# An attention step in another order, with its loads further ahead

## The chip, the cores and the metric

The kernel runs on one core of a Trainium2 chip. The metric is the device time of one execution in microseconds (us).

## The reference

An mLSTM cell and an expert layer follow each other. For 4 batches, 8 heads, 768 positions and head width 40, the cell carries a 40 x 40 matrix C, a vector n and a running maximum m:

```python
for t in range(S):
    m_new = np.maximum(f_gate[:, :, t] + m, i_gate[:, :, t])
    f_stab = np.exp(f_gate[:, :, t] + m - m_new)
    i_stab = np.exp(i_gate[:, :, t] - m_new)
    C = f_stab * C + i_stab * einsum('bhd,bhe->bhde', vt, kt)
    n = f_stab * n + i_stab * kt
    y[:, :, t] = sigmoid(o_gate[:, :, t]) * (C @ qt) / max(abs(n . qt), 1)
```

The cell's output, as 3072 rows of 320 values, goes through one of 8 experts per row, chosen by a hash of the row's token id:

```python
for e in range(8):
    mask = (token_ids * 2654435761) % 8 == e
    out[mask] = np.maximum(x[mask] @ w1[e], 0) @ w2[e]      # 320 -> 1024 -> 320
```

## The kernel before, in words

Attention works on tiles of 128 positions of one batch with all 8 heads: 6 chunks by 4 batches, 24 steps; step s has batch s % 4 and chunk s // 4. Inside a tile the recurrence is written as a masked product of scores and decays; between chunks C (with n as its 41st column) is carried, two buffers per batch. Each engine takes its instructions in the order in which the program issues them, and that order is written out by hand. Of a step there are these parts:

- `turn` (L300): four PE transposes of k, four of q, each into a PSUM tile of tag `tr`; ScalarE copies them to kT and qT, or VectorE in the step after a sigmoid.
- `decays` (L308): four matmuls of L with R (gate rows, loaded from DRAM) give the exponents `ab`, ScalarE takes their exponential into w; two more matmuls give `xb`, the decay of the row against the chunk's start, also in a `tr` tile; VectorE makes qs = qT * xb (L328), ScalarE copies the last column into `dec`.
- `decayed` (L358): GpSimd multiplies the old C by `dec` into the other buffer of C.
- `state` (L366): the update. PE makes k^T v into the last 164 columns of a PSUM tile `xh`, VectorE adds it to C (L381; in the first chunk a copy, L379).
- `k_weights` (L332): GpSimd makes kw, the weighted k of the update.
- `scores` (L346): 16 matmuls of kT and qT into two PSUM tiles; VectorE multiplies them into w (L354).
- `attend` (L383): the output. PE adds qs times the old C and w times v into the first 328 columns of the same `xh`; VectorE makes the denominators `den` from it (L402 to L404).
- `divided` (L406): VectorE divides into x. `gated` (L411): GpSimd multiplies x by the output gate, after a sigmoid over 8 steps at once (steps 5, 12 and 19). `store` (L415): to rows in DRAM.

In step s the order before is: decayed(s), divided(s-1), turn(s+2), decays(s+1), state(s), k_weights(s+1), scores(s+1), gated, attend(s). The gate preparation of chunks 1 to 4 (`g1`) hangs on steps 0 to 2, that of chunk 5 (`g2`) on steps 13 and 14. Routing hangs on the steps too, in `pieces`: iotas in 2 and 3, counts, totals, extra tiles, ranks and slots in 4 to 9, `route_hot` (one-hot tables on VectorE and GpSimd) in 10 to 17, `route_table` (six matmuls into `tk`, also a `tr` tile, and their sum into tv) in 12, 14, 16 and 18, and the index in 20. The first expert's weights are loaded on the way in seven slices, in the odd steps from 9 to 21.

PSUM has two buffers of tag `tr` in rotation, shared by the k and q turns, xb, tk and the small transposes; a new tile waits until the one before last has been read. SP issues nearly all loads, in order, and waits where a buffer isn't free: k and q are loaded 4 steps ahead into 4 buffers, v 3 ahead, and the gate rows R 2 ahead into 3.

Experts then follow on PE: gathers of rows on GpSimd, transposes, layer 1 (L760, L767), layer 2 (L796), a scatter. Each expert's weights are three tiles, with three buffers in `wpool` and in `w2pools[0]`; a second pool for w2 of three more is opened after attention, on the memory that attention gives back. Weights of expert 0 are loaded during attention, those of 1 and 2 on ScalarE's queue in the first expert.

Of the kernel before, what the change touches and what calls it, by code (L numbers as in the profile page):

```python
# [14 lines left out]
ALU = mybir.AluOpType  # L15
# [7 lines left out]
def kernel(  # L23
# [52 lines left out]
    consts = ctx.enter_context(tc.tile_pool(name="consts", bufs=1))  # L76
    wpool = ctx.enter_context(tc.tile_pool(name="wpool", bufs=3))
    w2pools = [ctx.enter_context(tc.tile_pool(name="w2pool", bufs=3))]

# [6 lines left out]

    def weights(src1, src2, w2pool, eng=None):
# [14 lines left out]
    def load_weights(e, eng=None):  # L102

        W[e] = weights(moe_w1[e], moe_w2[e], w2pools[e // 3 % 2], eng)

    def slices_of(e):

        w1t = wpool.tile([P, 2, F], F32, name="w1t")
        w1c = wpool.tile([P, FB // 2, P], F32, name="w1c")
# [21 lines left out]
    with tc.tile_pool(name="gates", bufs=1) as gp, \  # L131
# [5 lines left out]
        assert NB == 6 and BH == 32 and 3 * H <= 32 and DP == HB  # L137
        NG = 8
        ks = [gp.tile([P, H, DP], F32, name=f"k{i}") for i in range(4)]
        qs = [gp.tile([P, H, DP], F32, name=f"q{i}") for i in range(4)]  # L140
        vs = [gp.tile([P, H, D1], F32, name=f"v{i}") for i in range(4)]
        kws = [gp.tile([P, H, DP], F32, name=f"kw{i}") for i in range(2)]
        Cs = [[gp.tile([P, PR, 2, D1], F32, name=f"C{b}{i}") for i in range(2)] for b in range(B)]
        Ls = [gp.tile([P, B, P], BF16, name=f"L{i}") for i in range(2)]
        Lx = gp.tile([P, HB], BF16, name="Lx")
        Rs = [gp.tile([P, 2, H, P], BF16, name=f"R{i}") for i in range(3)]
        f_sb = gp.tile([BH, S], F32, name="f_sb")
# [21 lines left out]
        def load(s, what, eng=None):  # L169
            d = st.setdefault(s, {})  # L170
            eng = eng or nc.sync
            if what == "o":
                if s % NG == 0:
                    og[s // NG] = ld.tile([P, NG, H, D], F32, name="og", bufs=2)
                eng.dma_start(og[s // NG][:, s % NG], rows_of(o_gate, s))
            else:
                bufs, src = {"k": (ks, k), "q": (qs, q), "v": (vs, v)}[what]
                d[what] = bufs[s % 4]
                eng.dma_start(d[what][:, :, :D], rows_of(src, s))
# [6 lines left out]
        def load_a(s):  # L186
            n = 3 if s < B else 6
            src = pieces_of(s)[:, :n].rearrange("h i t -> i h t")
            for i in range(2):
                nc.sync.dma_start(Rs[s % 3][32 : 32 + n, i], src)  # L190

# [108 lines left out]
        def turn(s, what, on_act=True):  # L300
            d = st[s]
            d[what + "T"] = wk.tile([P, PR, P], F32, name=what + "T", bufs=3)
            tp = ps.tile([P, PR, P], F32, name="tr", tag="tr", bufs=2)
# [4 lines left out]
        def decays(s):  # L308
            b, c = place(s)
            d = st[s]  # L310
            R, L = Rs[s % 3], Ls[c % 2]
            w = d["w"] = wk.tile([P, 2, PR, P], F32, name="w")
# [70 lines left out]
        def attend(s):  # L383
# [4 lines left out]
            for j in range(PR):  # L388
# [6 lines left out]
                for hf in range(2):  # L395
                    for t in halves:
                        nc.tensor.matmul(  # L397
                            hs[t, 2 * j + hf, :], lhsT=d["w"][:, hf, j, t], rhs=d["v"][:, 2 * j + hf, :],
                            start=(c == 0), stop=True, skip_group_check=True,
                        )  # L400
            den = d["den"] = wk.tile([P, H, 1], F32, name="den")
            nc.vector.tensor_scalar(den[:], hs[:, :, D:], scalar1=-1.0, scalar2=1.0, op0=ALU.mult, op1=ALU.max)  # L402
            nc.vector.tensor_tensor(den[:], den[:], hs[:, :, D:], op=ALU.max)
            nc.vector.reciprocal(den[:], den[:])  # L404

        def divided(s):  # L406
            d = st[s]
            d["x"] = wk.tile([P, H, D], F32, name="x", bufs=8)
            nc.vector.tensor_tensor(d["x"][:], d["hs"][:, :, :D], d["den"][:].to_broadcast([P, H, D]), op=ALU.mult)

# [161 lines left out]
        def route_index():  # L572
# [11 lines left out]
            8: [lambda: route_beyond(CAP, b2), route_chosen], 9: [route_slots], 20: [route_index],  # L584
        }
        for i in range(NT // TH):
            pieces.setdefault(12 + 2 * i, []).append(lambda i=i: route_table(i))
        for i in range(2 * NT // TH):
# [29 lines left out]
        load_a(1)  # L618
        nc.vector.tensor_tensor_scan(m_sb[:, 1:], f_sb[:], i_sb[:], NEG, op0=ALU.add, op1=ALU.max)
        load(1, "v")  # L620
        load_a(2)
        for c in range(1, NB - 1):
            nc.sync.dma_start(m1[(c - 1) * BH : c * BH, :], m_sb[:, c * P : (c + 1) * P + 1])
        turn(1, "k")
        turn(1, "q")
        g0.weights(kwT0)
# [6 lines left out]
        nc.gpsimd.tensor_copy(Lx[:], one[:, 1].to_broadcast([P, HB]))  # L633
        load(3, "k")
        load(3, "q")
        load(2, "v")
        decays(0)
        scores(0)
        nsig, ndone, waiting = -1, 0, []
        for s in range(NT):  # L640
            b, c = place(s)
            if s + 2 < NT and s > 0:
                load_a(s + 2)
            if b == 2 and c < NB - 1:
                load_e(c + 1)
            if s + 4 < NT:
                load(s + 4, "k")
            if s + 3 < NT:
                load(s + 3, "v")
            for i in o_at.get(s, ()):  # L650
# [5 lines left out]
            waiting = []  # L656
            decayed(s)
            if s > 0:
                divided(s - 1)
            if s + 2 < NT:  # L660
                turn(s + 2, "k", s - 1 not in sig_at)
                turn(s + 2, "q", s - 1 not in sig_at)
            if s + 4 < NT:
                load(s + 4, "q")
            if s + 1 < NT:
                decays(s + 1)
            state(s)
            if s + 1 < NT:
                k_weights(s + 1)
                scores(s + 1)  # L670
            for i in range(2):
                if ndone < s and ndone // NG <= nsig:
                    gated(ndone)
                    waiting.append(ndone)
                    ndone += 1
            attend(s)
            if s in sig_at:
                nsig = sig_at[s]
                sigmoid(nsig)
            if s == 0:  # L680
                g1.sums(False)
                g1.split("A")
                g1.rows("A", nc.scalar.copy)
                nc.scalar.dma_start(z1[:, :3], g1.zt[:, :3])
            if s == 1:
                nc.scalar.activation(g1.t["X"][:, 0], g1.t["A"][:, 0], AF.Exp)
# [4 lines left out]
                g1.split("X")  # L691
                g1.rows("X", nc.scalar.copy)
                nc.scalar.dma_start(z1[:, 3:6], g1.zt[:, 3:6])
            if s == 2:
                g1.weights(kwT1)
            if s == 13:
                g2.sums(False)
                g2.split("A")
                g2.rows("A", nc.scalar.copy)
                g2.ends()  # L700
                g2.split("e")
                g2.rows("e", nc.scalar.copy)
            if s == 14:
                nc.scalar.activation(g2.t["X"][:, 0], g2.t["A"][:, 0], AF.Exp)
                g2.split("X")
                g2.rows("X", nc.scalar.copy)
                nc.scalar.dma_start(z2[:], g2.zt[:])
            for piece in pieces.get(s, []):
                piece()
        divided(NT - 1)  # L710
        while ndone < NT:
# [162 lines left out]
    with tc.If(nx > 0):  # L874
        with tc.For_i(0, nx, 1) as k:
# [5 lines left out]
                moe_w1[bass.ds(ex, 1)].rearrange("e d f -> (e d) f"),  # L881
                moe_w2[bass.ds(ex, 1)].rearrange("e f d -> (e f) d"), w2pools[0],
            )
# [37 lines left out]
```

## Time and profile before

| | |
|---|---|
| Time of three runs | 416.63, 416.9, 417.96 us (median 416.9) |
| The profiled execution's own time | 416.36 us |
| Its span in the trace | 414.6 us |
| PE busy | 371.1 us, 90% of the span |
| VectorE, ScalarE, GpSimd busy | 144.5, 104.6, 122.8 us |
| First output matmul of step 4 | 45.60 us from the span's start |
| First output matmul of step 23 | 149.77 us |
| First matmul of the experts | 165.79 us |

PE stands for the matmul engine, DVE for VectorE, ACT for ScalarE, POOL for GpSimd, SP for the engine that issues most DMAs. In the page's slices a digit is the busy share of a fortieth of the span in tenths. A row of the timeline has start, duration, engine, line, operation, output and inputs, the number of instructions merged, and in brackets how long the engine stood idle before it and who ended that. The chain of waits has start, duration and what ran. A row of stretches has its limits, its length, the busy time of PE, weight loads, DVE, ACT and POOL with the number of instructions, the clock granted to PE, the DMA engines' busy share and GB/s.

### The profile page before, as it was taken

Reading aid. Unit: us, or ns where it says so; the run is one execution under the profiler, and the core shown is the slowest. Engines: PE = TensorE matmul, PEld = TensorE weight load, DVE = VectorE, ACT = ScalarE, POOL = GpSimd, SP = SyncE. Lnnn points to the kernel's source line nnn. Section 1 sums busy time; section 2 is a strip of 40 time slices with the busy share of each in tenths; the row PEclk is TensorE's granted clock in tenths of the full one; section 3 lists DMA queues with packets and bytes.
Section 4 is the critical chain, followed back from the end, with each engine's and each line's share of the span. In section 5 each row is a group of like instructions: output and inputs, shape, how many; then the busy total and the mean of one; then the engine's idle time right before and its main releaser. Section 6 shows DMA issues by size and latency. Waiting matters only on the chain.

```text
span 414.6 us, 7819 instructions
## 1 busy us (share of the span) xinstructions
PE 371.1 (90%) x3124; PEld 251.8 (61%) x3124; DVE 144.5 (35%) x392; ACT 104.6 (25%) x203; POOL 122.8 (30%) x202
## 2 busy tenths in 40 slices
PE   4677998896899963999999999999999999999992
PEld 2565887785777751557566566556566565575561
DVE  8283888888777752110110200200200201101100
ACT  6334472464444810010110111110111110101100
POOL 5614255144762426301402313012313112010020
PEclk9996998999999995799999999999999999999997
DMA  7496987998399813998235254144254100000000
GB/s 148 79 171 129 178 149 152 206 200 158 79 213 191 212 68 96 300 288 268 63 112 174 79 171 146 32 144 148 61 171 146 33 17 30 0 32 17 0 18 32
DMA packets 125206, 50.91 MB, mean 123 GB/s; under 512 B 105164, under 2 KB 121424, under 8 KB 125168
## 3 DMA queue, kind: packets, MB, share of 16 engines
q1 hardware_dynamic: 117296, 36.36, 37.9%
q0 software_dynamic: 2496, 8.20, 6.4%
q10 hardware_dynamic: 5376, 5.84, 4.7%
q8 instruction: 25, 0.41, 0.4%
q14 instruction: 13, 0.11, 0.1%
HBM read 42.03 MB, written 8.61 MB: 122 GB/s over the span
## 4 chain that ended last, share of the span: by engine, by line
PE 71%; issue 8%; DVE 7%; POOL 5%; DMA 4%; ACT 2%; SPq 1%; POOLq 0%; ACTq 0%; DVEq 0%
PE mh L767 23%; PE zp L796 22%; PE mh L760 6%; PE xh L397 4%; PE tr L305 3%; PE sp L352 3%; PE xh L391 3%; PE ab L316 2%; POOL x L413 1%; PE tp L743 1%; PE xh L375 1%; PE zp L837 1%; DMA L<-gate_pieces 1%; POOL oh_c L554 1%; DMA R<-gate_pieces 1%
## 5 line engine op out<-in xcount | busy, mean ns | idle before, releaser
L796 PE MATMUL zp<-w2t,h 128*128 128x320 f32 x384 | 105.2, 433 | 0.0
L767 PE MATMUL mh<-xT,w1t 128*128 128x416 f32 x256 | 98.8, 530 | 0.9 <-POOL xT L829 0.9
L796 PEld LDWEIGHTS zp<-w2t,h 128*128 128x128 f32 x384 | 72.7, 190 | 32.1 <-issue 3.3
L767 PEld LDWEIGHTS mh<-xT,w1t 128*128 128x128 f32 x256 | 47.8, 194 | 44.0 <-issue 41.6
L749 DVE COPY xT<-tp 128x384 f32<-128x384 f32 x16 | 8.9, 558 | 142.3 <-PE tp L745 142.3
L730 POOL DMA_INDIRECT out_dram<-zo,s_idx x26 | 25.7, 987 | 92.5 <-ACT zo L729 92.5
L776 ACT ACTIVATE h<-mh 128x416 f32<-128x416 f32 x32 | 16.5, 517 | 110.0 <-PE mh L760 52.9
L774 DVE TENSOR_SCALAR h<-mh 128x416 f32<-128x416 f32 x32 | 18.9, 592 | 53.4 <-PE mh L760 26.9
L397 PE MATMUL xh<-v,w 128*64 128x41 f32 x768 | 34.7, 223 | 2.7 <-DVE C L379 2.7
L729 ACT COPY zo<-zp 128x320 f32<-128x320 f32 x26 | 11.1, 426 | 101.1 <-PE zp L796 92.9
L354 DVE TENSOR_TENSOR w<-sp,w 128x512 f32<-128x512 f32 x48 | 30.9, 686 | 15.4 <-PE sp L352 10.6
L397 PEld LDWEIGHTS xh<-v,w 128*64 128x64 f32 x768 | 30.5, 138 | 3.5 <-DVE C L379 3.1
L391 PE MATMUL xh<-C,qs 128*64 128x82 f32 x320 | 27.7, 252 | 4.3 <-DVE C L381 4.2
L352 PE MATMUL sp<-qT,kT 64*128 64x128 f32 x384 | 29.7, 297 | 0.0
L320 ACT ACTIVATE w<-ab 128x512 f32<-128x512 f32 x48 | 26.3, 606 | 7.4 <-PE ab L316 7.3
L868 POOL COPY hrem<-h 128x256 f32<-128x256 f32 x8 | 3.2, 400 | 84.1 <-ACT h L776 84.1
L760 PE MATMUL mh<-xT,w1c 64*128 64x416 f32 x128 | 26.7, 535 | 0.0
L352 PEld LDWEIGHTS sp<-qT,kT 64*128 64x128 f32 x384 | 24.9, 199 | 2.8 <-issue 1.0
L723 POOL DMA_INDIRECT xg<-x_rows,g_idx x24 | 23.4, 974 | 9.8 <-issue 9.8
L413 POOL TENSOR_TENSOR x<-x,og 128x320 f32<-128x320 f32 x24 | 20.4, 871 | 19.5 <-ACT og L344 11.4
L306 ACT COPY kT<-tr 128x512 f32<-128x512 f32 x21 | 12.3, 586 | 41.7 <-PE tr L305 40.5
L305 PE MATMUL tr<-ident,k 128*128 128x128 f32 x96 | 17.4, 310 | 5.2 <-DMA k<-in_k_dram 4.5
(170 smaller groups left out, 366.8 us busy)
## 6 DMA issues: line engine op xcount, KB each, us to landing
w2t<-in_moe_w_dram SPq DMA_DIRECT2D x5, 1280.0 KB
w1t<-in_moe_w_dram SPq DMA_DIRECT2D x5, 1024.0 KB
k<-in_k_dram SPq DMA_DIRECT2D x24, 160.0 KB
v<-in_v_dram SPq DMA_DIRECT2D x24, 160.0 KB
og<-in_o_gate_dram SPq DMA_DIRECT2D x24, 160.0 KB
x_rows<-x SPq DMA_DIRECT2D x24, 160.0 KB
q<-in_q_dram SPq DMA_DIRECT2D x23, 160.0 KB
w2t<-in_moe_w_dram ACTq DMA_DIRECT2D x2, 1280.0 KB
```

What stands on the lines that cost most here:

```text
L305: nc.tensor.transpose(tp[:, j, :], d[what][:, 2 * j : 2 * j + 2, :].rearrange("p h d -> p (h d)"), ident[:])
L320: nc.scalar.activation(w[:, hf], ab[:], AF.Exp)
L352: nc.tensor.matmul(sp[hf][:, j, :], lhsT=d["kT"][r, j, :], rhs=d["qT"][r, j, :], start=True, stop=True)
L354: nc.vector.tensor_tensor(d["w"][:, hf], sp[hf][:], d["w"][:, hf], op=ALU.mult)
L391: nc.tensor.matmul(d["xh"][t, 2 * j * D1 : (2 * j + 2) * D1], lhsT=d["qs"][:, j, t], rhs=Cs[b][c % 2][:, j].rearrange("p h d -> p (h d)"), ...
L397: nc.tensor.matmul(hs[t, 2 * j + hf, :], lhsT=d["w"][:, hf, j, t], rhs=d["v"][:, 2 * j + hf, :], start=(c == 0), stop=True, skip_group_che ...
L413: nc.gpsimd.tensor_tensor(x[:], x[:], og[s // NG][:, s % NG], op=ALU.mult)
L723: nc.gpsimd.indirect_dma_start(out=xg, out_offset=None, in_=x_d[:, :], in_offset=bass.IndirectOffsetOnAxis(ap=idx, axis=0),)
L730: ins = nc.gpsimd.indirect_dma_start(out=out[:, :], out_offset=bass.IndirectOffsetOnAxis(ap=idx, axis=0), in_=zo[:], in_offset=None, bound ...
L760: nc.tensor.matmul(hp[i][:, :cols], lhsT=w1c[r, fp, :], rhs=xT[r, 2, :cols], start=first, stop=not first,)
L767: nc.tensor.matmul(hp[i][:, :cols], lhsT=w1t[:, db, fb * P : (fb + 1) * P], rhs=xT[:, db, :cols], start=(first and db == 0), stop=(not fir ...
L796: nc.tensor.matmul(zp[:], lhsT=h[:, fb, j * P : (j + 1) * P], rhs=w[2][:, fb, :], start=(fb == 0), stop=(fb == FB - 1),)
```

## The change

Step s now runs turn(s+1), state(s), decays(s+1), k_weights(s+1), gated, decayed(s+1), attend(s), the routing piece, the denominators and divided(s), scores(s+1). The tables' matmuls come half a step earlier, after scores, in steps 11, 13, 15 and 17; the sigmoid is issued ahead of attend. The gates of chunks 1 to 4 make two of their three parts in step 0 and write them in one DMA; those of chunk 5 are spread over steps 12 to 14. k, q and v have 6 buffers and R has 4: k and q are loaded 5 steps ahead, v 4, R 3. The memory comes from the weight pools, which keep one buffer during attention; the others are opened after it. Turned k and q have 2 buffers instead of 3, x has 10 instead of 8.

```diff
-    wpool = ctx.enter_context(tc.tile_pool(name="wpool", bufs=3))
-    w2pools = [ctx.enter_context(tc.tile_pool(name="w2pool", bufs=3))]
+    wpools = [ctx.enter_context(tc.tile_pool(name="wpool", bufs=1))]
+    w2pools = [ctx.enter_context(tc.tile_pool(name="w2pool", bufs=1))]
...
-        W[e] = weights(moe_w1[e], moe_w2[e], w2pools[e // 3 % 2], eng)
+        W[e] = weights(moe_w1[e], moe_w2[e], wpools[e % 3 > 0], w2pools[e % 6 > 0], eng)
...
-        NG = 8
-        ks = [gp.tile([P, H, DP], F32, name=f"k{i}") for i in range(4)]
+        NG, KV = 8, 6
+        ks = [gp.tile([P, H, DP], F32, name=f"k{i}") for i in range(KV)]
...
-        Rs = [gp.tile([P, 2, H, P], BF16, name=f"R{i}") for i in range(3)]
+        Rs = [gp.tile([P, 2, H, P], BF16, name=f"R{i}") for i in range(4)]
...
-            d[what + "T"] = wk.tile([P, PR, P], F32, name=what + "T", bufs=3)
+            d[what + "T"] = wk.tile([P, PR, P], F32, name=what + "T")
...
+        def divided(s):
+            d = st[s]
+            hs = d["hs"]
             den = d["den"] = wk.tile([P, H, 1], F32, name="den")
...
-        def divided(s):
-            d = st[s]
-            d["x"] = wk.tile([P, H, D], F32, name="x", bufs=8)
+            d["x"] = wk.tile([P, H, D], F32, name="x", bufs=10)
...
+        products = {}
         for i in range(NT // TH):
-            pieces.setdefault(12 + 2 * i, []).append(lambda i=i: route_table(i))
+            products[11 + 2 * i] = [lambda i=i: route_table(i)]
...
+        nc.vector.tensor_copy(Rs[3][:], Rs[1][:])
...
-        turn(1, "k")
-        turn(1, "q")
...
-        load(3, "k")
-        load(3, "q")
-        load(2, "v")
+        for i in range(3, KV - 1):
+            load(i, "k")
+            load(i, "q")
+            load(i - 1, "v")
...
-            if s + 2 < NT and s > 0:
-                load_a(s + 2)
+            if s + 3 < NT and s != 1:
+                load_a(s + 3)
             if b == 2 and c < NB - 1:
                 load_e(c + 1)
-            if s + 4 < NT:
-                load(s + 4, "k")
-            if s + 3 < NT:
-                load(s + 3, "v")
+            if s + KV - 1 < NT:
+                load(s + KV - 1, "k")
+                load(s + KV - 1, "q")
+            if s + KV - 2 < NT:
+                load(s + KV - 2, "v")
+            if s == 1:
+                load_a(s + 3)
...
-            decayed(s)
-            if s > 0:
-                divided(s - 1)
-            if s + 2 < NT:
-                turn(s + 2, "k", s - 1 not in sig_at)
-                turn(s + 2, "q", s - 1 not in sig_at)
-            if s + 4 < NT:
-                load(s + 4, "q")
+            if s + 1 < NT:
+                turn(s + 1, "k", s - 1 not in sig_at)
+                turn(s + 1, "q", s - 1 not in sig_at)
+            state(s)
             if s + 1 < NT:
                 decays(s + 1)
-            state(s)
-            if s + 1 < NT:
                 k_weights(s + 1)
-                scores(s + 1)
...
-            attend(s)
+            if s + 1 < NT:
+                decayed(s + 1)
             if s in sig_at:
                 nsig = sig_at[s]
                 sigmoid(nsig)
+            attend(s)
+            for piece in pieces.get(s, []):
+                piece()
+            divided(s)
+            if s + 1 < NT:
+                scores(s + 1)
             if s == 0:
                 g1.sums(False)
+                nc.scalar.activation(g1.t["X"][:, 0], g1.t["A"][:, 0], AF.Exp)
                 g1.split("A")
                 g1.rows("A", nc.scalar.copy)
-                nc.scalar.dma_start(z1[:, :3], g1.zt[:, :3])
+                g1.split("X")
+                g1.rows("X", nc.scalar.copy)
+                nc.scalar.dma_start(z1[:, :6], g1.zt[:, :6])
...
-            if s == 13:
+            if s == 12:
                 g2.sums(False)
+                nc.scalar.activation(g2.t["X"][:, 0], g2.t["A"][:, 0], AF.Exp)
                 g2.split("A")
                 g2.rows("A", nc.scalar.copy)
+            if s == 13:
+                g2.split("X")
+                g2.rows("X", nc.scalar.copy)
+            if s == 14:
                 g2.ends()
                 g2.split("e")
                 g2.rows("e", nc.scalar.copy)
...
-            for piece in pieces.get(s, []):
+            for piece in products.get(s, []):
                 piece()
-        divided(NT - 1)
...
-    w2pools.append(ctx.enter_context(tc.tile_pool(name="w2late", bufs=3)))
+    wpools.append(ctx.enter_context(tc.tile_pool(name="wlate", bufs=2)))
+    w2pools.append(ctx.enter_context(tc.tile_pool(name="w2late", bufs=5)))
```

More of the change, by code (lines that the diff above doesn't have):

```diff
@@ L85, with weights @@
     xe = consts.tile([1, NX + 1], I32, name="xe")
-    def weights(src1, src2, w2pool, eng=None):
+    def weights(src1, src2, wpool, w2pool, eng=None):
         eng = eng or nc.sync
@@ L102, in load_weights @@
     def load_weights(e, eng=None):
-        W[e] = weights(moe_w1[e], moe_w2[e], w2pools[e // 3 % 2], eng)
+        W[e] = weights(moe_w1[e], moe_w2[e], wpools[e % 3 > 0], w2pools[e % 6 > 0], eng)
     def slices_of(e):
-        w1t = wpool.tile([P, 2, F], F32, name="w1t")
-        w1c = wpool.tile([P, FB // 2, P], F32, name="w1c")
+        w1t = wpools[0].tile([P, 2, F], F32, name="w1t")
+        w1c = wpools[0].tile([P, FB // 2, P], F32, name="w1c")
         w2t = w2pools[0].tile([P, FB, Dm], F32, name="w2t")
@@ L137 @@
         assert NB == 6 and BH == 32 and 3 * H <= 32 and DP == HB
-        NG = 8
-        ks = [gp.tile([P, H, DP], F32, name=f"k{i}") for i in range(4)]
-        qs = [gp.tile([P, H, DP], F32, name=f"q{i}") for i in range(4)]
-        vs = [gp.tile([P, H, D1], F32, name=f"v{i}") for i in range(4)]
+        NG, KV = 8, 6
+        ks = [gp.tile([P, H, DP], F32, name=f"k{i}") for i in range(KV)]
+        qs = [gp.tile([P, H, DP], F32, name=f"q{i}") for i in range(KV)]
+        vs = [gp.tile([P, H, D1], F32, name=f"v{i}") for i in range(KV)]
         kws = [gp.tile([P, H, DP], F32, name=f"kw{i}") for i in range(2)]
@@ L177, in load @@
                 bufs, src = {"k": (ks, k), "q": (qs, q), "v": (vs, v)}[what]
-                d[what] = bufs[s % 4]
+                d[what] = bufs[s % KV]
                 eng.dma_start(d[what][:, :, :D], rows_of(src, s))
@@ L189, in load_a @@
             for i in range(2):
-                nc.sync.dma_start(Rs[s % 3][32 : 32 + n, i], src)
+                nc.sync.dma_start(Rs[s % 4][32 : 32 + n, i], src)
         def load_e(c, b0=0):
@@ L310, in decays @@
             d = st[s]
-            R, L = Rs[s % 3], Ls[c % 2]
+            R, L = Rs[s % 4], Ls[c % 2]
             w = d["w"] = wk.tile([P, 2, PR, P], F32, name="w")
@@ L404, in attend @@
             nc.vector.reciprocal(den[:], den[:])
-        def divided(s):
-            d = st[s]
-            d["x"] = wk.tile([P, H, D], F32, name="x", bufs=8)
-            nc.vector.tensor_tensor(d["x"][:], d["hs"][:, :, :D], d["den"][:].to_broadcast([P, H, D]), op=ALU.mult)
+            d["x"] = wk.tile([P, H, D], F32, name="x", bufs=10)
+            nc.vector.tensor_tensor(d["x"][:], hs[:, :, :D], den[:].to_broadcast([P, H, D]), op=ALU.mult)
         def gated(s):
@@ L679 @@
                 sigmoid(nsig)
+            attend(s)
[4 more added lines that the diff above has]
+                scores(s + 1)
             if s == 0:
                 g1.sums(False)
+                nc.scalar.activation(g1.t["X"][:, 0], g1.t["A"][:, 0], AF.Exp)
                 g1.split("A")
                 g1.rows("A", nc.scalar.copy)
-                nc.scalar.dma_start(z1[:, :3], g1.zt[:, :3])
+                g1.split("X")
+                g1.rows("X", nc.scalar.copy)
+                nc.scalar.dma_start(z1[:, :6], g1.zt[:, :6])
             if s == 1:
-                nc.scalar.activation(g1.t["X"][:, 0], g1.t["A"][:, 0], AF.Exp)
                 g1.ends()
@@ L690 @@
                 nc.scalar.dma_start(z1[:, 6:], g1.zt[:, 6:])
-                g1.split("X")
-                g1.rows("X", nc.scalar.copy)
-                nc.scalar.dma_start(z1[:, 3:6], g1.zt[:, 3:6])
             if s == 2:
                 g1.weights(kwT1)
-            if s == 13:
+            if s == 12:
                 g2.sums(False)
+                nc.scalar.activation(g2.t["X"][:, 0], g2.t["A"][:, 0], AF.Exp)
                 g2.split("A")
                 g2.rows("A", nc.scalar.copy)
+            if s == 13:
+                g2.split("X")
+                g2.rows("X", nc.scalar.copy)
+            if s == 14:
                 g2.ends()
@@ L702 @@
                 g2.rows("e", nc.scalar.copy)
[L703 to L706, printed above, removed]
                 nc.scalar.dma_start(z2[:], g2.zt[:])
-            for piece in pieces.get(s, []):
+            for piece in products.get(s, []):
                 piece()
-        divided(NT - 1)
         while ndone < NT:
@@ L881 @@
                 moe_w1[bass.ds(ex, 1)].rearrange("e d f -> (e d) f"),
-                moe_w2[bass.ds(ex, 1)].rearrange("e f d -> (e f) d"), w2pools[0],
+                moe_w2[bass.ds(ex, 1)].rearrange("e f d -> (e f) d"), wpools[0], w2pools[0],
             )
```

## The prediction

> **What bounds the kernel now.** I read the page's slices first, to find the stage that the change touches.
>
> ```profile
> PE   4677998896899963999999999999999999999992
> DVE  8283888888777752110110200200200201101100
> DMA  7496987998399813998235254144254100000000
> ```
>
> A slice is 10.4 us. PE carries slices 16 to 40 (experts) alone; the edit leaves that work as it is. In slices 2 to 15 (attention) PE, DVE and the DMA engines are all nearly full: no one bound, but a loop of steps in which each engine waits for the others in turn. So I took the PE rows of one step from the timeline, and the chain of waits where steps were long.
>
> ```profile
> 47.23 0.66 PE L305 MATMUL tr<-ident,k 128*128 128x128 f32 x4
> 47.72 0.60 PE L305 MATMUL tr<-ident,q 128*128 128x128 f32 x4
> 48.25 0.62 PE L316 MATMUL ab<-R,L 128*64 128x512 bf16 x4
> 48.71 0.38 PE L324 MATMUL xb<-R,Lx 128*64 128x512 bf16 x2
> 48.93 0.61 PE L375 MATMUL xh<-v,kw 128*64 128x41 f32 x16
> 49.47 1.16 PE L352 MATMUL sp<-qT,kT 64*128 64x128 f32 x16
> 51.18 0.36 PE L391 MATMUL xh<-C,qs 128*64 128x82 f32 x4 [0.55 <-DVE C L381]
> ```
>
> From start to start: turns 1.02 us, exponents 0.46, row decay 0.22, update 0.54, scores 1.09 (44.51 to 45.60), output 1.63 (45.60 to 47.23): 4.96 us of PE, which is the period of the quick steps. The last row shows that the output waits for DVE's addition to C (L381), though it reads another C: both lie in the tile xh. It starts 0.06 us after that addition ends, wherever it waits. In the steps with one-hot tables the addition itself waits for GpSimd:
>
> ```profile
> 83.52 0.27 DVE oh_c L549
> 83.86 0.67 POOL oh_c L554
> 84.61 0.43 POOL oh_c L554
> 85.03 0.70 POOL C L361
> 85.75 0.32 DVE C L381
> 86.09 0.34 DVE C L381
> 86.47 0.36 PE xh L391 x4
> ```
>
> Near the end a gate row is late:
>
> ```profile
> 118.07 3.68 DMA R<-gate_pieces
> 130.49 2.49 DMA L<-gate_pieces
> ```
>
> **A rule for a step, tested on before.** Let A be the start of a step's first output matmul. DVE then runs den at A+1.75 (0.60 to the next), the routing piece p, x (0.40), qs (0.60), the addition (0.65); the output follows 0.06 later, or PE at 4.96. For p = 1.99 (step 8, 72.40 to 74.39) this gives 6.04, measured 5.95; for 3.07 (step 6) 7.1, measured 7.03; for 1.21 (step 9) 5.25, measured 5.17. The DVE rows explain the periods to 0.1 us; the cover for p is some 0.7 us.
>
> **The change, part by part.** PE's order becomes output(s), scores(s+1), turns(s+2), update(s+1), exponents, row decay, output(s+1). DVE's: qs, piece, den, x (all inside or just behind the output), product w (L354), addition. From A: scores begin at 1.63, w 1.26 later (45.77 against 44.51) at 2.89, and 1.20 on the addition could start, at 4.09. But scores end at 2.72, turns at 3.74, the update's last matmul at 4.35, the addition starts 0.12 later (19.29 against 19.16), 4.47 to 5.12, and the output at 5.18. So a light step costs 5.18 against 4.96: **0.22 lost on every light step**. In return a piece has more cover: qs takes A to A+0.57, den and x need 1.04 ahead of 2.89, which leaves 1.28 (was 0.7).
>
> The decay of C moves ahead of the one-hot products on GpSimd, so those two leave the addition's path. Pieces over 1.28 still delay w. What now sits between w and the addition counts in full: the second gate set (1.54 in step 12, 0.47 in 13, 1.14 in 14; rows 100.21 to 103.11 and 108.17), and the kT and qT copies that DVE takes after a sigmoid (1.20). The four token tables (tk) now follow the scores; their sums tv (0.4) wait behind w, end at 4.5, and the q turn needs tk's PSUM buffer (two "tr" buffers in rotation; before, the row at 109.16 waits likewise 0.73). Then q turn 4.6, update to 5.7, output at 6.53: **1.35 more than a light step, four times**. Loads, one step further ahead with six buffers, I cost at nothing: SP issues some 4.5 us per step, and the bulk packets (5,121 of 160 bytes in 40 to 45 us, four loads of 1,024 a step) need about 4 us. If that cover fails, 17 and 19 keep their late rows (rival three). At nothing too go the small edits: four more memsets of k and q (0.26 each, on GpSimd ahead of kw(1), which nobody needs before 22), the copy of a fourth R (0.67 on DVE at 9.9, ahead of kwT0's, while PE waits for L until 13.8), one DMA less on ScalarE's queue. The weights of experts 1 and 2 now lie where attention's tiles lay; ScalarE issues them in the first expert, after 165.8, and every reader of those tiles is done at 153.6 (last gate product, 152.69 + 0.86); expert 1 needs them some 30 us later. If a wait stood there, ScalarE's relu (L776) would queue behind it, and PE behind that.
>
> Periods from A(s) to A(s+1), before as measured, after by this rule:
>
> ```
> s       4    5    6    7    8    9   10   11   12   13
> before 5.57 5.41 7.03 6.53 5.95 5.17 5.21 5.21 6.27 7.96
> after  5.18 6.57 6.59 5.48 5.51 5.18 5.18 6.53 7.54 7.00
> s      14   15   16   17   18   19   20   21   22   sum
> before 6.31 5.21 6.64 5.21 6.13 4.95 4.52 3.37 1.52 104.17
> after  5.94 6.53 5.18 6.53 5.18 5.05 4.42 4.42 4.24 108.25
> ```
>
> Steps 6, 7, 8 hold pieces of 3.07, 1.96, 1.99: w starts at 1.61 + p, and the output 1.91 later. Step 5: the totals' matmuls (0.36) go ahead of den, so w ends at 4.66, then the copies 1.20, addition, 6.57. Step 12: 4.09 + 1.54 + 1.20 + 0.65 + 0.06. Step 13: tv behind the split, q turn at 5.08, output 7.00. Step 14: 4.09 + 1.14 + 0.71. From 19 on there is no update. Step 22 ends in a wait for w: 2.89 + 1.29 + 0.06.
>
> The loop itself is thus 4.1 us longer; 2.1 of it is only one turn and one score set that before has done earlier, 1.5 the wait for the last w.
>
> *Start.* Before, A(4) is at 45.60. After, step by step: turns(1) fall into step 0, w(1) ends at 23.0; first gate set's sums and splits (now A and X) 23.0 to 25.1, addition(1), A(1) = 25.85; qT(2) is copied behind the gate rows on ScalarE until 27.15, scores(2) to 28.3, w(2), e pieces to 30.7; A(2) = 31.4 to 32.2; kT(3), qT(3) until 32.75, scores(3) to 34, kwT1's transpose and its copy at 35.6, which frees the buffer for the q turn; update(3) 36.6, exponents(4) 37.1 if their rows are there. A(3) = 37.5 to 37.9 and, with 4.61 (1.06 + 1.09 + 1.02 + 0.61 + 0.83), A(4) = 42.0 to 42.5. L for step 4 is issued behind 16 bulk loads (13 before): from 17.0 at 0.98 us each, landing 36.5 to 38.1. I take A(4) = **42.6**, 3.0 earlier; bounds 41.9 and 45.0.
>
> Last output: 42.6 + 108.25 = 150.85 against 149.77 before: **+1.1**. Behind it x, gate, store, gathers and experts are the same rows.
>
> *Clock.* The windows show it halving after 3.41 us with PE only 41% or 45% busy, and not after 57%:
>
> ```profile
> 31.00:34.42 3.42, 1.41 (x35) 1.29 (x36) 1.43 (x4) 2.69 (x6) 0.00 (x0) 1.00 0.30 81
> 34.42:41.25 6.83, 6.15 (x49) 4.42 (x47) 2.54 (x9) 2.42 (x5) 4.20 (x17) 0.50 0.89 152
> 99.27:102.69 3.42, 1.95 (x25) 1.37 (x21) 2.82 (x13) 0.51 (x1) 0.00 (x0) 1.00 0.36 70
> ```
>
> In step 12 after, PE idles 4.74 to 6.35 and 6.57 to 7.54, 2.6 us inside 2.8: for some two thirds of the possible places of the window's edge it is under half busy, and the next 3.41 us run at half speed, 1.7 us lost, some 0.3 of it under other waits: **+1.4**; bounds 0 and 3 (a second one in step 13). The Trainium skill ("TensorE: Matmul & The Clock Gate", Part 1) has the clock fall only after an idle window of about 3.4 us. By that rule this term would be 0 and the sum +1.1; the rows above, where PE was at work 41% of the window, speak for the harsher reading. The skill also speaks against deeper bulk loads ahead of small ones ("DMA: Bandwidth & Descriptors", Queues, rings and completion order): each DMA engine takes a ring's descriptors in order. The trace agrees in kind: L took 1.58 us at 12.13 with little ahead, R 3.68 at 118.07 behind a weight slice. By that rule L would land behind all 16 loads, at the late end, and the sum would be some 0.7 higher.
>
> Sum: +1.1 + 1.4 = +2.5 on the profiled execution's 416.36, 418.9; that execution stood 0.5 under the median of 416.9, so 419.4.
>
> **Rivals.** *One, faster:* the output doesn't wait for the addition in the new order. Then light steps take 4.96 and the steps where DVE is last lose the 0.65: 4, 9, 10, 16, 18 save 1.1, the table steps 0.5, steps 7 and 8 1.0, and 5, 6, 12, 13, 14 3.8: 6.4 in all, to 411.6 without a clock loss. For it: nothing reads what the addition writes. Against it: the 0.06 after each addition, also in steps with no old C (25.39 behind 25.33).
>
> *Two, slower:* the gate rows of step 4 stand behind the bulk loads and PE idles long enough for a half clock there: A(4) = 45.0 in place of 42.6, 421.8. It decides once exponents(4) start over 1 us after 37.1. For it: DMA 1.02 busy in 27.59 to 31.00; against it: SP halts for the gate pieces and lets the loads run off.
>
> *Three, the depth does nothing:* DMA engines, 0.65 to 0.91 busy per 20 us, limit steps 16 to 19, and the 1.9 and 1.4 us of late rows stay: 422.7. Against it: in slice 11 (104 to 114) they are busy 3 tenths only, so there is room to run ahead.
>
> **How the numbers follow.** Forecast 0.50, one 0.20, two 0.20, three 0.10. A measurement of this kernel tells 0.3%, 1.25 us, from no change. The forecast's own range is 415.4 to 422.9 (earliest start and no clock loss, or a second half window, and 0.1 us on each of 19 steps); of its 0.50, 0.06 fall faster, 0.13 within, 0.31 slower. Rival one gives 0.17 faster, 0.03 within; two 0.02 within, 0.18 slower; three 0.01 and 0.09. Faster 0.23, within 0.19, slower 0.58. The range of 8 in 10 reaches from most of rival one to most of three: 412 to 423.5.
>
> **What would show it.** Right: no POOL C row on the chain; no R or L wait after 110; in light steps a wait of about 0.2 of L391 for L381; q turns waiting near 1 us behind tv after each table; A(4) near 42.6 and the last output near 151. Wrong: outputs that start with no DVE addition just ahead; light periods of 4.96 or over 5.4; exponents(4) waiting for L; a period in steps 6 to 8 no shorter than before.

## The result, and the profile after

The changed kernel takes 433.11 us (median of 4 runs, 430.48 to 439.15), the kernel before on the same chip 416.79 us: a ratio of 1.036, 95% interval 1.031 to 1.042. Ratios, here and below, leave out runs over 1.5% above the fastest of the same kernel (here the one of 439.15). It is slower by 16 us, and the forecast of 419.4 (412.0 to 423.5) is missed. The profiled execution took 430.48 us with a span of 428.7, against 416.36 and 414.6. Slices of the page after:

```profile
PE   2677887886869885499999999999999999999992
DVE  7375899978767684211020120110110210201100
DMA  7477989896059831399517218235216101000000
```

A slice is 10.7 us. PE's steady nines (the experts) begin in slice 18, one later than before, and of the slices 1 to 16 one holds a 9, where there were six. The DMA row holds a 0 and a 5 in slices 11 and 12, in the middle of attention: there the loads stop. The first output matmul of step 4 starts at 45.45 us (before 45.60), that of step 23 at 164.11 (149.77), and behind it the two executions are alike: 430.48 - 164.11 = 266.4 against 416.36 - 149.77 = 266.6. The loss lies wholly in the steps from 4 on.

A light step (16) in the timeline of PE after, to be read against the rows of step 4 before:

```profile
127.85 0.36 PE L391 MATMUL xh<-C,qs 128*64 128x82 f32 x4 [0.18 <-DVE C L381]
...
129.48 1.16 PE L352 MATMUL sp<-qT,kT 64*128 64x128 f32 x16
130.57 0.66 PE L305 MATMUL tr<-ident,k 128*128 128x128 f32 x4
131.06 0.60 PE L305 MATMUL tr<-ident,q 128*128 128x128 f32 x4
131.59 0.67 PE L375 MATMUL xh<-v,kw 128*64 128x41 f32 x16
132.08 0.61 PE L316 MATMUL ab<-R,L 128*64 128x512 bf16 x4
132.52 0.39 PE L324 MATMUL xb<-R,Lx 128*64 128x512 bf16 x2
133.09 0.36 PE L391 MATMUL xh<-C,qs 128*64 128x82 f32 x4 [0.18 <-DVE C L381]
```

That is the order forecast, with the forecast wait of 0.2 us for the addition; the period is 5.24 (forecast 5.18). So the order is not the surprise. PE's waits in attention after (us in total, times, longest) show what else there is:

```profile
PE xh L391 <- DVE C L381: 9.9, 14, 2.3
PE xb L324 <- DVE kT L306: 3.2, 2, 2.7
PE ab L316 <- DMA L<-gate_pieces: 3.1, 2, 1.6
```

A wait of 2.3 for an addition whose own work is 0.65 means that VectorE came late to it, and exponents wait twice, up to 1.6, for gate rows L. Two causes stand behind these waits.

**VectorE stops beside GpSimd.** VectorE is busy 156.0 us, 144.5 before; the same groups of instructions take 9.9 us longer (0.7 of it is the copy into the fourth R). Two small operations of step 4 before, and then the same step of the changed kernel, VectorE's and GpSimd's rows together:

```profile
48.21 0.17 DVE L466 TENSOR_SCALAR ei<-tok 128x24 int32<-128x24 int32 x1
...
48.41 0.18 DVE L467 CAST ef<-ei 128x24 f32<-128x24 int32 x1
```

```profile
46.39 0.73 POOL L361 TENSOR_TENSOR C<-C,dec 128x328 f32<-128x328 f32 x1 [0.44 <-ACT dec L330]
...
46.42 0.73 DVE L467 TENSOR_SCALAR ei<-tok 128x24 int32<-128x24 int32 x1
...
47.08 0.72 POOL L338 TENSOR_TENSOR kw<-k,kwT 128x320 f32<-128x320 f32 x1
47.19 0.65 DVE L468 CAST ef<-ei 128x24 f32<-128x24 int32 x1
```

In the changed kernel each starts just behind the start of a GpSimd product and ends just behind its end: 47.15 and 47.12, 47.83 and 47.80. The new order puts `decayed` and `k_weights` of the next step (GpSimd) at the very place where the routing pieces stand (VectorE). Not every operation suffers: the products w<-sp,w, with an operand in PSUM, took 0.686 us in the 21 that overlapped such a product and 0.683 in the 27 that did not; den, x, qs and the additions were the same within 0.01 too. Nor does every operation from memory to memory: the reciprocal of den took 0.203 us beside 11 products and 0.203 in the 13 without, and a sum along a row (xe_f, 61.78) kept its 0.317 inside a gate product. Those held up are sums, products and comparisons of two operands, scans, casts and operations with a constant.

**SP stops behind another engine's write.** Timeline rows of SP (its queue) and of ScalarE's queue:

```profile
101.66 0.66 SPq L179 DMA_DIRECT2D v<-in_v_dram  x1
...
119.93 0.32 ACTq L712 DMA_DIRECT2D gate_pieces<-zt  x1
...
121.60 0.37 SPq L175 DMA_DIRECT2D og<-in_o_gate_dram  x1
```

SP stands still for 19.3 us of the 19.9 between its two rows. The load at 121.60 fetches an output gate; it reads nothing of the gate pieces. In the semaphore events it waits on semaphore 106, which is the one that ScalarE's write of the chunk-5 gate pieces (119.93, landed 121.58) counts up: in this program the loads of SP and the writes of ScalarE take their completion semaphores in turn from one set of eight numbers (100, 102 to 108), and whoever gets a number waits until its last holder has landed. SP's waits in the changed kernel (first line) and in the kernel before (second line), and SP's rows around the stop in the kernel before:

```profile
SPq L175 <- DMA gate_pieces<-zt: 22.8, 2, 19.3
```

```profile
SPq L179 <- DMA gate_pieces<-zt: 7.3, 1, 7.3
```

```profile
102.60 1.17 SPq L418 DMA_DIRECT2D x_rows<-x  x2
111.04 0.38 SPq L179 DMA_DIRECT2D q<-in_q_dram  x1
```

So the stop was there before, with 7.3 us. The write stands in step 14 in both kernels; in the changed one that step's first output begins 7.5 us later (113.40, before 105.91), the write is issued 6.5 us behind it in place of 3.4, and SP, a step further ahead, stops 1.5 us earlier: together 19.3. Everything that SP issues behind it is late.

### The profile page after: what moved, and what is told of

The parts are those of the page before. It is cut to its first block, busy times and chain, and to the rows that moved or that the text cites. A ratio compares the mean times of both kernels' runs of the same rounds, so it can differ in the third digit from the quotient of the medians.

```text
span 428.7 us, 7871 instructions
## 1 busy us (share of the span) xinstructions
PE 370.6 (86%) x3124; PEld 248.5 (58%) x3124; DVE 156.0 (36%) x393; ACT 106.3 (25%) x203; POOL 124.8 (29%) x208
## 4 chain that ended last, share of the span: by engine, by line
PE 66%; issue 13%; DVE 9%; POOL 4%; DMA 3%; ACT 2%; SPq 0%; POOLq 0%; ACTq 0%; DVEq 0%
PE mh L772 22%; PE zp L801 21%; PE mh L765 6%; PE sp L352 4%; PE tr L305 3%; PE xh L397 3%; PE xh L391 2%; PE xh L375 2%; DVE C L381 2%; POOL x L414 1%; DVE w L354 1%; PE tp L748 1%; PE zp L842 1%; PE ab L316 1%; POOL out_dram L735 1%
## 5 line engine op out<-in xcount | busy, mean ns | idle before, releaser
L772 PE MATMUL mh<-xT,w1t 128*128 128x416 f32 x256 | 97.7, 526 | 0.9 <-POOL xT L834 0.9
L397 PE MATMUL xh<-v,w 128*64 128x41 f32 x768 | 35.9, 226 | 4.9 <-DVE C L379 2.9
L397 PEld LDWEIGHTS xh<-v,w 128*64 128x64 f32 x768 | 31.6, 140 | 7.5 <-DVE C L379 4.8
L352 PE MATMUL sp<-qT,kT 64*128 64x128 f32 x384 | 30.6, 304 | 0.3 <-ACT qT L306 0.3
L361 POOL TENSOR_TENSOR C<-C,dec 128x328 f32<-128x328 f32 x16 | 13.6, 849 | 51.7 <-ACT dec L330 51.7
L391 PEld LDWEIGHTS xh<-C,qs 128*64 128x64 f32 x320 | 17.0, 139 | 16.8 <-DVE C L381 16.2
```

What stands on the lines that cost most here:

```text
L352: nc.tensor.matmul(sp[hf][:, j, :], lhsT=d["kT"][r, j, :], rhs=d["qT"][r, j, :], start=True, stop=True)
L391: nc.tensor.matmul(d["xh"][t, 2 * j * D1 : (2 * j + 2) * D1], lhsT=d["qs"][:, j, t], rhs=Cs[b][c % 2][:, j].rearrange("p h d -> p (h d)"), ...
L397: nc.tensor.matmul(hs[t, 2 * j + hf, :], lhsT=d["w"][:, hf, j, t], rhs=d["v"][:, 2 * j + hf, :], start=(c == 0), stop=True, skip_group_che ...
L772: nc.tensor.matmul(hp[i][:, :cols], lhsT=w1t[:, db, fb * P : (fb + 1) * P], rhs=xT[:, db, :cols], start=(first and db == 0), stop=(not fir ...
```

## Experiments

Twelve kernels ran, on three chips where the kernel before took 418.1, 418.7 and 418.7 us; ratios are to those.

**The two halves of the change.** The order alone keeps the pools and distances of before:

```diff
-        NG, KV = 8, 6
+        NG, KV = 8, 4
...
-            if s + 3 < NT and s != 1:
-                load_a(s + 3)
+            if s + 2 < NT and s > 0:
+                load_a(s + 2)
```

> The changed kernel's order with the loads, buffers and pools of before (k and q 4 ahead, v 3, R 2). Theory 'order': the loss is in the step itself, VectorE's routing pieces now running beside GpSimd's decay and kw products (the 0.17 us mask of L467 took 0.73 us in the changed kernel's trace, ending with a GpSimd product). Then the loss stays: 426 to 436 us, VectorE busy near 155 us. Theory 'depth': SP running further ahead is what hurts (it stands 19.3 us until the last gate pieces land). Then this is near before, 415 to 421 us, and VectorE's busy time falls back.

Measured 431.73 us, 1.031 (1.028 to 1.035). VectorE's groups are 8.6 us longer than before, and SP's longest wait for the gate pieces is 13.5 us: both causes come with the order alone, though at this depth no exponents wait longer than 0.6 us for rows and step 18 takes 5.24.

The depth alone keeps the order of before and takes buffers and distances from the changed kernel (the reverse of the diff above).

> Before's order with the changed kernel's buffers, pools and load distances. Theory 'order': no loss here, 412 to 418 us (the late gate rows of steps 17 and 19, 1.9 and 1.4 us, may go). Theory 'depth': slower than before by 4 us or more, 421 to 432 us.

Measured 423.06 us, 1.011 (1.008 to 1.014): the depth, which I had costed at nothing, loses 1.1% by itself. VectorE is only 1.0 us longer (0.7 of it the copy into the fourth R); SP's and PE's waits in it say why, the longest of PE's in step 18, which takes 11.48 (6.13 before) with the clock halved from 137.83 to 144.66:

```profile
SPq L179 <- DMA gate_pieces<-zt: 17.2, 3, 11.9
...
PE ab L316 <- DMA L<-gate_pieces: 6.4, 2, 3.8
```

**The shared semaphore.** To take the wait away without touching the data, the gate pieces are written from GpSimd's queue, whose DMAs have semaphores of their own (111 to 118):

```diff
-                nc.scalar.dma_start(z2[:], g2.zt[:])
+                nc.gpsimd.dma_start(z2[:], g2.zt[:])
```

and so for the writes of z1. First in the changed kernel, then in the one before, then in the one with depth alone:

> The changed kernel with the writes of the gate pieces of chunks 1 to 5 issued from GpSimd's queue instead of ScalarE's, nothing else. Theory 'shared semaphore': SP's loads stood 3.5, 1.9 and 19.3 us until a write from ScalarE's queue had landed, without needing its data; those waits go, L for step 4 lands by 38 instead of 40.1, step 18 no longer waits for L, and the time falls by 3 to 5 us. Theory 'order only': SP's waits cost nothing, the time stays within 1.5 us.

> The same move in the kernel before: the gate pieces of chunks 1 to 5 written from GpSimd's queue. Theory 'shared semaphore': SP's stop of 7.3 us at 103.8 goes, and with it the late rows of steps 17 and 19 (1.9 and 1.4 us): 412 to 415 us. Rival: those rows are late because SP's issues and the weight slices fill the queue; then within 1 us of 416.8.

> Before's order, the changed kernel's depths, and the gate pieces of chunks 1 to 5 written from GpSimd's queue. Theory 'shared semaphore': the 4.7 us that depth alone lost (SP stood 17.2 us for those writes, PE 6.4 us for L) come back, 413 to 417 us. Rival 'bulk ahead of rows': the rows stay behind the bulk loads in the queue and the loss stays, 420 us or more.

Measured 431.32 us, 1.030 (1.026 to 1.034); 414.19, 0.992 (0.989 to 0.994); 414.0, 0.989 (0.984 to 0.993). In the second only the gate rows, which do read the pieces, still wait for them (2.8 us at most), the 7.3 us are gone, and steps 16 and 18 take 5.62 us each in place of 6.64 and 6.13. In the third the whole loss of the depth is gone, and nothing is gained over the second: the theory of the shared semaphore holds, and the depth has nothing to give once the stop is away. In the changed kernel it gave less than I expected: 1.030 in place of 1.036, and these two intervals overlap. Step 18 does fall from 6.63 to 5.24, but the first output of step 4 comes at 46.88 (45.45), and step 15 rises from 6.70 to 9.34. PE is 32% busy there from 125.13 to 128.54, and then runs at half clock until 131.96. The rows ahead of it show the other cause at its worst, since the GpSimd work that waits behind the write now meets a one-hot table:

```profile
123.30 1.68 POOL L414 TENSOR_TENSOR x<-x,og 128x320 f32<-128x320 f32 x2
123.39 2.45 DVE L550 TENSOR_TENSOR oh_c<-iota_f,rc 128x141 bf16<-128x141 f32 x1
...
124.94 0.72 POOL L361 TENSOR_TENSOR C<-C,dec 128x328 f32<-128x328 f32 x1
...
127.14 0.29 PE L566 MATMUL tk<-oh_c,oh_r 128*128 128x94 bf16 x3 [1.66 <-POOL oh_c L555]
```

An operation of 0.3 us lasts through three products, 2.45 us, and PE waits 1.66 for what follows from it.

**VectorE beside GpSimd.** GpSimd's products of decay, kw and the output gate are cut to one or two columns, so that they hold GpSimd only 0.2 us; the rest of each product is left out. In the changed kernel and in the one before:

```diff
-                    d["kw"][:, :, :D], d["k"][:, :, :D],
+                    d["kw"][:, :, :1], d["k"][:, :, :1],
...
-            nc.gpsimd.tensor_tensor(x[:], x[:], og[s // NG][:, s % NG], op=ALU.mult)
+            nc.gpsimd.tensor_tensor(x[:, :, :1], x[:, :, :1], og[s // NG][:, s % NG][:, :, :1], op=ALU.mult)
```

> The changed kernel with GpSimd's decay, kw and gate products cut to one or two columns per head (the rest of these products is left out); instructions, order and waits stay. Theory 'two engines at one port': VectorE's pieces that read and write SBUF alone stop while GpSimd computes; cut, they take before's times (ei and ef 0.17 us instead of 0.73 and 0.65, the g2 scan 0.41 instead of 1.10), VectorE's busy time falls from 156 to 147 us or less, the periods of steps 4, 6 to 9, 12 and 14 fall by 0.4 to 1.8 us each, and the time is 419 to 426 us. Rival 'long loop': the order of the engines' turns costs the time whatever GpSimd does; the time falls by less than 3 us, to 429 to 433.

> The same cut in the kernel before, as a control. Theory 'port': there GpSimd's products lie mostly beside VectorE work on PSUM; its busy time falls by 2 us at most and the time by 1 to 3 us (the decay of C is on the path in steps 10 to 17). If it fell by as much as in the changed kernel, GpSimd's mere length would be the cause, not the new overlap.

Measured 423.05 us, 1.007 (1.003 to 1.011), and 413.77, 0.988 (0.984 to 0.993). In the changed kernel VectorE's groups are 9.88 us shorter, as much as the change had added; in the kernel before they are 2.10 shorter. About 3% of the time goes with it in the new order, 1.2% in the old one (more than the 1 to 3 us I had expected of it, since shorter products also let their readers start earlier).

A complete kernel on the same lines moves only the decay away from GpSimd, as four ScalarE products a step (0.28 us each):

```diff
-                nc.gpsimd.tensor_tensor(
-                    Cs[b][(c + 1) % 2].rearrange("p j h d -> p j (h d)"), ...
+                for j in range(PR):
+                    nc.scalar.activation(
+                        Cs[b][(c + 1) % 2][:, j].rearrange("p h d -> p (h d)"), ...
+                        AF.Copy, scale=st[s]["dec"][:, j, :],
```

> The changed kernel, complete, with the decay of C as four products on ScalarE in place of GpSimd's one. Theory 'port': GpSimd's kw and gate products stay, so only part of the overlap goes: VectorE's busy time falls from 156 to 150 to 153 us and the time to 427 to 431. Rival 'long loop': unchanged at 432 to 434, or slower by ScalarE's longer step.

Measured 430.59 us, 1.022 (1.013 to 1.032): VectorE's groups are 5.7 us shorter. Part of the stop is moved, not removed: the sum slot<-slot,gx falls from 0.84 to 0.36, but gx<-gx,b rises from 0.36 to 0.90 beside another product.

**Both at once.** The changed kernel with small products and the gates by GpSimd:

> The changed kernel with both suspected costs taken away at once: GpSimd's products cut to one or two columns (the rest of decay, of the keys' update weights and of the output gate is left out) and the gate rows' writes issued from GpSimd's queue instead of ScalarE's. If these two are the whole loss: the steps 4 to 8 take 5.2 to 6.6 us and so do 12 to 18, the loads are issued with waits under 3 us for the gate rows, the last output begins at 145 to 152 us and the time is 408 to 415 us, about that of the kernel before with small products (413.8). If the new order has a cost of its own beside them (the output behind the update, the light steps of 5.2 us): 416 to 422 us.

Measured 419.81 us, 1.005 (1.001 to 1.008), in the second case, in which the new order has a price of its own; the last output, at 149.85, lies in the range of the first. Its profiled run took 416.96, the shortest of its seven. Step 4 of its timeline, the same four instructions as above:

```profile
44.19 0.20 POOL L361 TENSOR_TENSOR C<-C,dec 128x8 f32<-128x8 f32 x1 [1.48 <-ACT dec L330]
...
44.22 0.20 DVE L467 TENSOR_SCALAR ei<-tok 128x24 int32<-128x24 int32 x1
44.35 0.21 POOL L338 TENSOR_TENSOR kw<-k,kwT 128x8 f32<-128x8 f32 x1
...
44.46 0.18 DVE L468 CAST ef<-ei 128x24 f32<-128x24 int32 x1
```

The order is untouched and GpSimd's products still run beside the pieces, but they are short, and ei and ef are back at 0.20 and 0.18. PE's wait for the addition has its number of times, and half its sum:

```profile
PE xh L391 <- DVE C L381: 4.7, 14, 0.8
```

The periods from one step's first output matmul to the next's, as forecast, in the changed kernel, and here:

```
s          4    5    6    7    8    9   10   11   12   13
forecast 5.18 6.57 6.59 5.48 5.51 5.18 5.18 6.53 7.54 7.00
after    6.27 6.54 7.33 6.52 6.62 5.59 5.24 6.44 8.76 8.64
neither  5.28 6.53 5.85 5.26 5.59 5.24 5.25 6.42 7.63 7.18
s         14   15   16   17   18   19   20   21   22   sum
forecast 5.94 6.53 5.18 6.53 5.18 5.05 4.42 4.42 4.24 108.25
after    7.75 6.70 5.24 6.43 6.63 5.02 4.39 5.88 2.67 118.66
neither  6.60 6.40 5.24 6.42 5.24 5.05 4.39 4.36 2.67 106.60
```

With neither cause the forecast table comes out within 0.13 us in 14 of the 19 steps. Step 6 is shorter than forecast because og (L486) no longer meets a product, and step 22 because step 23's output begins without waiting for the last w and waits for it inside (0.6 and 0.3 us). Against the kernel before with small products (413.6 in its profiled run) 3.4 us remain: 2.2 of it up to the last output (its first matmul at 149.85 against 147.66), the rest behind it. The medians stand 6.0 apart (419.8 and 413.8). That is the order's own price, and if anything it is higher, since the kernel before with small products still had SP's stop; the kernel before with neither was not run. The other runs of the changed kernel with neither took 418.9 to 421.7; what they lost against the profiled one no trace shows, and that stays open.

The complete kernels with both remedies, gates by GpSimd and decay on ScalarE, in the changed kernel, in the order of before with depth, and in the kernel before:

> The changed kernel, complete, with the decay as four ScalarE products and the gate rows' writes issued from GpSimd's queue. Theory of the two causes: it takes away most of the loads' waits and about 6 of the 10 us that VectorE lost to GpSimd's products, so 417 to 425 us, well below the 433 of the changed kernel and the 430 to 431 of each remedy alone. If only the start is late for a reason of its own: 428 to 431 us.

> The order of before, the loads further ahead, the gate rows' writes from GpSimd's queue, and the decay as four ScalarE products of 0.28 us. By depth with the gate rows by GpSimd alone 414.0 us; the ScalarE decay frees VectorE and GpSimd but adds 1.1 us of ScalarE to a step: 411 to 415 us if VectorE's overlap with GpSimd matters in the old order (small products gave 4 to 5 us), 415 to 420 if ScalarE is then late with the weights of the scores.

> The kernel before with the gate rows' writes from GpSimd's queue and the decay as four ScalarE products. Gate rows alone gave 414.2 us; expected 411 to 415 us, above 416 if ScalarE's 1.1 us a step are on the path.

Measured 425.28 us, 1.018 (1.014 to 1.021); 417.67, 0.998 (0.994 to 1.001); 415.25, 0.993 (0.990 to 0.996). The first lies just above its expectation: the remedies nearly add up (1.022 and 1.030 each alone), but GpSimd's kw and gate products remain. The second is worse than the same without ScalarE's decay (414.0), the miss that I had named: its row decay (xb) waits up to 3.8 us for a copy on ScalarE (2.8 without), and PE ran at half clock from 104.6 to 111.4. The third gains nothing over gates by GpSimd alone (414.2). Why is not shown; in the old order there was little overlap to remove, and the decay gives ScalarE 1.1 us more in a step.

The fastest complete versions are thus the kernel before, with or without the depth, and its gate pieces written from GpSimd's queue: 0.992 and 0.989, with overlapping intervals (and 0.993 with the decay on ScalarE too).

## Why the prediction was wrong

*Right:* the light step (forecast 5.18, measured 5.24 in 10 and 16), the token tables (6.53; 6.44, 6.70 and 6.43), the step after a sigmoid (5, forecast 6.57, measured 6.54), the wait of the output for an addition in the same tile, so no rival one. The chain of waits shows the table step in the order foretold: scores, table, k turn, then the q turn behind a copy, and no decay of C in it.

```profile
91.26 1.09 PE sp L352 x16
92.35 0.37 PE tk L566 x6
92.72 0.47 PE tr L305 x4
...
93.27 0.59 ACT kT L306
...
93.91 0.66 PE tr L305 x4
```

The table's size is right and its reason is not: the q turn was to wait for the sums tv, and it starts 0.06 us behind the kT copy, ahead of the end of the second sum (93.91 against 94.09); in step 17 it is the same. And the decay of C, which was to leave the chain, stands on it three times elsewhere (122.49, 134.08, 140.52; 2.6 us together).

Right too, in this execution, was the clock term. Stretches of the changed kernel (limits, length, busy times of PE, weight loads, VectorE, ScalarE, GpSimd, granted clock, DMA share, GB/s):

```profile
23.77:27.19 3.42, 0.89 (x30) 0.90 (x32) 2.35 (x7) 1.84 (x5) 1.90 (x9) 1.00 0.97 172
...
102.27:105.69 3.42, 1.34 (x30) 1.04 (x31) 3.34 (x9) 1.64 (x4) 0.20 (x1) 1.00 0.65 115
105.69:109.11 3.42, 3.42 (x45) 3.12 (x42) 1.44 (x6) 0.00 (x0) 3.29 (x6) 0.50 0.02 5
119.35:122.76 3.41, 1.83 (x52) 1.73 (x51) 1.89 (x6) 2.63 (x6) 0.27 (x1) 1.00 0.11 25
```

The gates' step left PE busy in 39% of a window (1.34 of 3.42), and the next ran at half clock, as forecast; 54% busy (119.35) cost nothing. Step 13 is 1.64 over the table, which is that term's 1.4 and little more (with neither cause, at full clock, it is 0.18 over). The clock falls here after windows in which PE was far from idle, so the harsher reading taken in the prediction stands and the idle-window rule does not. Where the windows fall is luck: with neither cause, no window behind 30.29 ran at half clock in attention.

*The step that failed first* is the price of the pieces: "what now sits between w and the addition counts in full", with "rows 100.21 to 103.11" for durations, and the pieces p. I moved VectorE's work to another place and kept the durations that it had beside an idle GpSimd, while moving GpSimd's products to the same place. By rows, in the changed kernel: step 4 lost 0.56 + 0.47 on ei and ef, and is 1.09 over the forecast; step 12 lost 0.69 on the scan A_zt (1.10 against 0.41) and 0.49 on the next sum, and is 1.22 over; steps 6, 7 and 8 lose 0.74, 1.04 and 1.11 with b, gx and slot in the same way. Step 14 is 1.81 over; with neither cause still 0.66, since ScalarE's zt copy stands ahead of the kT copy that the row decay xb waits for, which I had not queued. The trace of before showed the mechanism in one place, its timeline at 23 us, where I did not look at durations of one instruction side by side:

```profile
23.23 0.29 DVE L275 TENSOR_TENSOR A_zt<-A_zt 128x128 f32<-128x128 f32 x1
...
23.49 0.72 POOL L338 TENSOR_TENSOR kw<-k,kwT 128x320 f32<-128x320 f32 x1 [3.51 <-PE xh L375]
23.56 0.80 DVE L276 TENSOR_TENSOR A_zt<-A_zt 128x128 f32<-128x128 f32 x1
```

Two sums of the same size, one 0.29 us, the other 0.80 because it begins 0.07 behind a GpSimd product. Even the 3.07 us of the piece in step 6 held such a row (og 0.95, in the changed kernel 0.33). The Trainium skill ("SBUF — State Buffer", SBUF: two separate sides) states a rule that would have spoken against this change: VectorE and GpSimd share one pair of memory ports; between a GpSimd operation that reads that memory, as the products here do, and a VectorE operation that has two operands in it or runs in a two-port performance mode, whoever starts first holds the pair for the whole instruction, and the other is blocked. These rows agree (0.17 to 0.73, ending with the product), also in its bound, that an operation of two operands of which one lies in PSUM is not held up (w 0.686 and 0.683). In which mode ei and ef ran no trace shows.

*The second failed step:* "Loads, one step further ahead with six buffers, I cost at nothing: SP issues some 4.5 us per step". I summed what SP does and not what it waits for. The 7.3 us of the kernel before were in its list of waits; I read its late R (3.68 at 118.07) as a load "behind a weight slice". With the gates written from GpSimd's queue these waits are gone behind step 4 in the order of before, at both depths: they were the stop's. In the changed kernel it is worth the 1.45 of step 18. Where the forecast said "no R or L wait after 110", L is 1.57 late at 145.50. Rival three had the late rows staying, but for want of DMA engines; these lay idle in slice 11 (0 tenths).

*The start* failed by both: A(4) was forecast at 42.6, bounds 41.9 and 45.0, and came at 45.45. The gates' scan at 23.66 took 0.82 in place of 0.42, a window with PE 26% busy brought two windows of half clock (27.19 to 34.02), and L was issued at 37.59 to 38.55, after SP had waited 3.5 us at an output gate and 1.9 at gate rows for the first writes of the pieces, in place of landing at 36.5 to 38.1:

```profile
38.26 1.86 DMA L<-gate_pieces
...
40.16 0.62 PE ab L316 x4
```

With neither cause A(4) is 43.25, but with the gates' writes alone moved it is 46.88: there SP waits up to 5.0 us for the pieces that L itself reads, and issues L at 37.89. So only the run with both causes gone shows that they made the start late. Rival two's place was right, and its price too, but not its reason: L was not slow behind bulk packets, it was issued late.

The sum: start +2.85, steps 4 to 9 +4.36, 12 to 14 +4.67 (of which 1.4 was forecast as the clock), 18 +1.45, 21 +1.46, 22 -1.57, the others +0.04 together; 164.11 - 150.85 = 13.3. Step 21 is the first cause again, as ta and g_idx of step 20's index beside three gate products took 0.69 to 0.79 in place of 0.14 to 0.19; that step 22 offsets it is luck, for it came out at 2.67 with neither cause too. Taking the clock's 1.4 off and the 0.2 behind the last output gives 11.6, the miss of the profiled execution (430.48 against 418.9). How much of it is each cause's comes from the ratios: small products take 1.036 to 1.007, the gates' queue 1.036 to 1.030, both to 1.005, where the forecast was 1.006. That last agreement flatters: short products also help the kernel before by 1.2%, and against it so shortened the new order costs 3.4 to 6.0 us, not the 2.5 forecast. What the rest of that is stays open.

## What to carry to other kernels

When work is moved on one engine, its duration moves with it only if the other engines at the new place are the same: lay VectorE's and GpSimd's rows of the new order side by side, and price at that product's end each VectorE operation from memory to memory that starts beside a GpSimd product, if it is of a kind that a trace shows held (here all but the reciprocal and the sum along a row). Look through the list of waits for a queue that waits for a transfer whose data it does not need: a late small write on one queue can hold another queue's loads, and more depth makes that stop longer, not shorter; moving it to a third queue is an edit of one word in each of a few lines and was worth 0.8%. An order that PE fills well is worth nothing if its gaps were chosen with another engine's old durations.

## What the runs showed of the hardware

VectorE does not slow down beside GpSimd, it stops: 0.17 us became 0.73, 0.30 became 2.45 through three products in a row, while operations with a PSUM operand, the reciprocal of den (0.203 either way) and a sum along a row (0.317) were not touched. The stop goes both ways at times: two gate products at 60.62, beside such an operation, took 1.85 us, 1.68 elsewhere. In the changed kernel TensorE's half clock came after windows with PE 26% and 39% busy and not after 54% or 57%; the border is not sharp, for in the kernel before with small products it came after one with 55% (1.89 of 3.41 us from 28.20). The changed kernel's profiled run had 6.8 + 3.4 us of half clock in attention, the run with the gates by GpSimd 6.8 + 3.4 + 3.4 + 6.8 + 3.4, though it waited less for loads.
